# Halving the first and last unit by queries, maxima as bf16 trees, and eight-head projections spread by DMA, in a two-branch attention kernel

## The chip, the core and the metric

The kernel runs on one core of one Trainium2 chip. A core has five engines, each with its own instruction stream: TensorE (PE in the profile, its weight loads PEld), VectorE (DVE), ScalarE (ACT), GpSimd (POOL) and SyncE (SP), whose stream here only issues DMAs. Operands lie in SBUF; TensorE writes its products to PSUM, eight banks of 128×512 f32. The metric is the device time of one execution in microseconds (us), as the median of several; smaller is better.

## The reference

Two independent attention branches of 32 heads with 16 dimensions each, sequence S = 2048, width 512, bf16 inputs; their outputs are concatenated.

```python
# A: softmax attention
q, k, v = split_heads(x @ wqkv)                  # 32 heads, 16 dimensions
p = softmax(einsum("bhqd,bhkd->bhqk", q, k) * 16 ** -0.5)
a = merge(einsum("bhqk,bhkd->bhqd", p, v)) @ wo
# B: linear attention with a learnt feature map
q, k, v = split_heads(x2 @ wqkv2)
pq, pk = q @ w_phi, k @ w_phi                    # per head, 16 x 16
phi_q = concat([softmax(pq), softmax(-pq)])      # 32 features; phi_k alike
kv, z = phi_k^T v, sum_s(phi_k)
b = merge((phi_q kv) / (phi_q z + 1e-6)) @ wo2
out = concatenate([a, b], axis=-1)
```

Branch A forms 32 score maps of 2048×2048. Branch B never forms a score map; its softmax over 16 features needs, for each position and head, the largest and the smallest of 16 values.

## The kernel before

The heads of A go in eight groups `g` of four. A head's 16 dimensions are padded to 32 rows, so four heads fill the 128 rows of a column block of `QT` and `KT` (both `[128, group, S]`). A unit `u = (g, c)` is one group with one block `c` of 512 queries: 32 units, `c` outermost. Each unit is computed in two passes.

*First pass, the maxima.* A unit has 32 steps. A step is two matmuls of `emit_m1` (L889), which write scores of two heads for 128 queries by 512 keys into two of PSUM's banks 0 to 3, and one reduction r1 of `emit_r1` (L903), by which DVE takes the maximum over the 512 keys of each. When a segment's steps are done, `emit_mchain` reduces the four partial maxima (L913, DVE), POOL negates them and splits them into a high and a low bf16 half (L918, L920, L921), SP transposes them by a DMA into `mcols` (L923) and copies them by two DMAs into rows 16 and 17 of each head in `QT` (L926). The same rows of `KT` hold ones, so that the second pass subtracts the maximum inside its matmul.

*Second pass, the exponentials.* Eight steps after its end (`LAGX`), a segment's blocks begin, 64 for a whole unit: a block is one score matmul M2 of one head, 128 keys by 512 queries, into one of the three ring banks 4 to 6 (L954), and one exponential of ScalarE from PSUM into a slot of `pT` (L960, 15 slots). Four blocks later `pv_go` multiplies by V with a column of ones (L1008, four column groups of TensorE, bank 7), so that the sums of the exponentials come out beside the products. After a unit, ScalarE evacuates bank 7 to `X`, and SP and POOL form reciprocals (L1117 DMA, L1122 power on POOL, DMAs L1124 and L1127) and multiply (L1137) into `QT`, which serves as storage of the normalised output; later jobs project it with `WOp` (L820) and store it.

A unit in `SPLIT` (0 and 31) goes as two segments of two heads with all 512 queries. In PV each such segment fills only two column groups; in unit 0, 64 matmuls of zeros fill the others, and in the last unit additional matmuls with ones make the sums (64 rows × 512 columns each).

*Projections.* `proj` projects x for one group and one 512-block (L457), four matmuls with zero-padded weights `WQp`, `WKp`, which DVE fills at the start by two memsets (L304, L305) and two copies (`pad_copy`, L312). ScalarE evacuates into `KT` with a bias that sets the rows of ones (L469), or into `QT` (L433). Groups 2 to 7 need 24 K jobs and 6 Q jobs from slot 30 on, every four slots; the Q jobs of the other query blocks follow from slot 200, every 16.

*Branch B* runs as background jobs. `fm(n)`, n = 0 to 31, starts at slot 172 + 26n: 128 positions of the 512 features of K (n below 16) or Q. The job's matmuls (L583) are evacuated by ScalarE to `pB` (L433, f32), `red` takes maximum and minimum on DVE (L593, L596), `sub` subtracts both on POOL (L603, L605), ScalarE exponentiates (L611), POOL sums (L618 to L629), takes reciprocals by a power (`rec`, L641) and multiplies (L661); matmuls, transposes, a power for the denominators (L769) and the output copy L800 follow.

*What sets the order.* A planner, written in Python, simulates the engines with fixed costs (the class `_Clock`, its object `ck`) and lays down each engine's instruction order. In each turn it picks a step, a block, a piece of a background job (`jobs`, each with a first slot and a due slot `by`), a PV, or matmuls of zeros (L1086, L1101), which keep TensorE busy. `later(slot, fn)` runs `fn` at a given step; `pool_slot` keeps POOL free around a segment's end; `ck.extra` charges DVE for work beside r1. Waits are semaphores derived from the dependencies. SP takes its instructions in order: a DMA that has to wait for its data holds up what follows it.

*The end.* After the last r1 come the remaining blocks. `emit_acc` lays down, seven matmuls at a time, the projection of seven groups of the last four output tiles (L1152); before the last unit's normalisation three bursts stand in the planned order without a place in the planner's time, the fourth is in `emit_last`. That function then forms reciprocals as exp(−ln(sum)) on ScalarE (L1167, L1171), multiplies on DVE (L1176), adds the eighth group (L1183) and stores (L1191).

Of the kernel before, what the change touches and what calls it, by code (L numbers as in the profile page):

```python
# [148 lines left out]
def bass_concat_heads__softmax_full_mha__linear_kernel_hedgehog__prompt_kernel(  # L149
# [7 lines left out]
    NG = 8  # L157
# [4 lines left out]
    SPLIT = {0, NU - 1}  # L162
# [20 lines left out]
    for u in range(NU):  # L183
        segs += [(u, (0, 1)), (u, (2, 3))] if u in SPLIT else [(u, (0, 1, 2, 3))]
# [3 lines left out]
    for v, (u, rows) in enumerate(segs):  # L188
        steps = [(v, rows[i] // 2, qt, kc) for kc in range(NKC) for qt in range(4) for i in range(0, len(rows), 2)]
        if u == 0 and v == 1:  # L190
            order[4:4] = steps[0:4]
            steps = steps[4:]
        order += steps
    steps_of = [[q for q, o in enumerate(order) if o[0] == v] for v in range(NV)]
    seg_end = [qs[-1] + 1 for qs in steps_of]
    of_b = [v for v in range(NV) for _ in range(NKT * len(segs[v][1]))]
    seg_b = [of_b.index(v) for v in range(NV)]
    LAG = seg_end[0] + LAGX

    with contextlib.ExitStack() as es:  # L200
# [33 lines left out]
        WQp = sb("WQp", [128, 4, NG, 128], BF)  # L234
        WKp = sb("WKp", [128, 4, NG, 128], BF)
# [15 lines left out]
        pB = sb("pB", [128, 2, 512], F32)  # L251
# [3 lines left out]
        mB = sb("mB", [128, 2, 2, 32], F32)  # L255
# [48 lines left out]
        t_wq0 = P.op("dve", lambda e: e.memset(wqf.bitcast(U32), 0))  # L304
        t_wk0 = P.op("dve", lambda e: e.memset(wkf.bitcast(U32), 0))  # L305
# [3 lines left out]
        def pad_copy(dst, col0, dep0):  # L309
            src = wA[:, :, col0:col0 + 512].rearrange("p ct (gr d) -> p ct gr d", d=16)  # L310
            dv = dst[:].rearrange("p ct g (r x) -> p ct (g r) x", x=32)[:, :, :, 0:16]
            return P.op("dve", lambda e: e.tensor_copy(dv, src), [t_wa[col0 // 512], dep0])  # L312

# [3 lines left out]
        t_stage0 = P.op("pool", lambda e: e.memset(flat(stage).bitcast(U32), 0), [t_wkp])  # L317
        t_bd0 = P.op("pool", lambda e: e.memset(flat(BD).bitcast(U32), 0))
        t_wo0 = P.op("pool", lambda e: e.memset(flat(WOp).bitcast(U32), 0))
        t_vp1 = P.op("pool", lambda e: e.memset(VP[:, :, :, 16:17], 1.0))  # L320
        t_yd1 = P.op("pool", lambda e: e.memset(Yd[:], 1.0))
        t_vb1 = P.op("pool", lambda e: e.memset(vB[:], 1.0))
# [37 lines left out]
        def add_job(slot, pieces, fin, by=None, when=None):  # L360
            by = slot + BY if by is None else by
            njobs[0] += 1
            jobs.append((by, slot, njobs[0], pieces, fin, when))

        def next_job(tau):

            return min((j for j in jobs if j[1] <= tau and (j[5] is None or j[5]())), default=None)
# [9 lines left out]
        def bg_at(tau):  # L377
# [5 lines left out]
            if j is None or not ring_free:  # L383
                return None
# [941 lines left out]
```

## Time and profile before

| what | value |
|---|---|
| median of 3 runs | 1284.21 us (1283.9 to 1286.1) |
| the profiled execution's own time | 1283.74 us |
| its span, first to last instruction | 1282.0 us |
| TensorE's granted clock | 0.998 |
| VectorE busy | 1214.9 us, 95%, of it r1 (L903) 1170.2 |
| ScalarE busy | 1180.3 us, 92%, of it exponentials (L960) 1062.0 |
| TensorE busy | 1219.7 us, 95%, of it matmuls of zeros 581.9 + 146.7 |
| GpSimd busy | 600.8 us, 47% |
| DMA | 26.69 MB, 21 GB/s on average |

The page of the profile gives for one execution each engine's busy time with its share of the span, a strip of 40 slices with the busy share in tenths, and the costliest groups of instructions, one line each: source line and engine, operation, output<-inputs with partitions × elements, the count; then the busy time and the mean of one in ns; then the engine's idle time just ahead of these instructions and what ended most of it. Timelines list instructions in order of time: start, duration, engine, line, and in square brackets the idle time before with its releaser. SPq is SyncE's DMA queue.

### The profile page before, as it was taken

To read this page: it belongs to the slowest core of one execution; us is meant where nothing else is said; L and a number is where in the kernel's file an instruction comes from. 1 tells how busy PE (TensorE), PEld (TensorE's weight loads), DVE (VectorE), ACT (ScalarE), POOL (GpSimd) and SP (SyncE) were. 2 spreads that over 40 slices of the span, in tenths; PEclk is the share of its full clock that TensorE was granted. 3 is DMA by queue.
4 is the path that set the end of the run, shared out by engine and by line. 5 is a ranking of instruction groups with operands and counts; after the bars stand their busy time and mean duration, and the time that the engine had idled before them with its cause. 6 is when DMAs were issued, how large, how long until landed. Compare 5 with 4: busy or idle time off the path is not lost.

```text
span 1282.0 us, 28798 instructions
## 1 busy us (share of the span) xinstructions
PE 1219.7 (95%) x12059; PEld 408.0 (32%) x12059; DVE 1214.9 (95%) x1132; ACT 1180.3 (92%) x2321; POOL 600.8 (47%) x620
## 2 busy tenths in 40 slices
PE   8999999999999999999999999999999999999998
PEld 2223333333332233333333333333333233333333
DVE  8999999999999999999999999999999999999920
ACT  3789999999998999999999899999999999999986
POOL 2000102544655565546646346556555554646640
PEclk9999999999999999999999999999999999999999
DMA  6212200000001000000001110112211202121110
GB/s 132 60 16 40 35 7 4 7 7 7 7 6 19 6 8 7 7 6 3 7 7 7 23 24 11 31 19 20 32 19 27 36 15 32 23 24 19 29 20 21
DMA packets 75209, 26.69 MB, mean 21 GB/s; under 512 B 65928, under 2 KB 73096, under 8 KB 75080
## 3 DMA queue, kind: packets, MB, share of 16 engines
q1 hardware_dynamic: 73736, 23.56, 13.6%
q8 instruction: 94, 1.54, 0.5%
q10 hardware_dynamic: 1344, 1.31, 0.3%
q14 instruction: 35, 0.29, 0.1%
HBM read 3.16 MB, written 4.19 MB: 6 GB/s over the span
## 4 chain that ended last, share of the span: by engine, by line
ACT 51%; PE 27%; DVE 21%; issue 1%; DMA 0%; SPq 0%; ACTq 0%
ACT pT L960 45%; DVE part L903 20%; PE PS L954 7%; PE PS L889 4%; PE PS L457 3%; PE PS L1101 3%; PE PS L1008 2%; PE PS L583 2%; ACT eB L611 1%; PE PS L445 1%; PE PS L793 1%; PE PS L684 1%; ACT X L433 1%; ACT pB L433 1%; PE PS L1152 1%
## 5 line engine op out<-in xcount | busy, mean ns | idle before, releaser
L903 DVE TENSOR_REDUCE part<-PS 128x2 f32<-128x1024 f32 x1024 | 1170.2, 1215 | 5.7 <-PE PS L889 2.2
L960 ACT ACTIVATE pT<-PS 128x512 bf16<-128x512 f32 x2048 | 1062.0, 637 | 67.2 <-PE PS L954 27.0
L954 PE MATMUL PS<-QT,KT 32*128 32x512 bf16 x2048 | 657.1, 384 | 18.1 <-ACT pT L960 2.6
L1086 PE MATMUL PS<-zmv,ones_t 32*128 32x512 bf16 x1745 | 581.9, 382 | 0.3 <-ACT X L433 0.2
L889 PE MATMUL PS<-KT,QT 32*128 32x512 bf16 x2048 | 447.3, 383 | 14.1 <-DVE part L903 10.6
L954 PEld LDWEIGHTS PS<-QT,KT 32*128 32x128 bf16 x2048 | 176.9, 91 | 400.0 <-ACT pT L960 243.7
L1008 PE MATMUL PS<-pT,VP 128*17 128x512 bf16 x2048 | 210.7, 384 | 9.9 <-ACT pT L960 0.8
L918 POOL TENSOR_SCALAR stage<-mrow 128x16 bf16<-128x16 f32 (+1 forms) x34 | 8.8, 259 | 332.9 <-DVE mrow L913 332.9
L1101 PE MATMUL PS<-zmv,ones_t 128*17 128x256 bf16 x3028 | 146.7, 276 | 1.5
L1086 PEld LDWEIGHTS PS<-zmv,ones_t 32*128 32x128 bf16 x1745 | 143.3, 91 | 1.7 <-ACT X L433 1.1
L889 PEld LDWEIGHTS PS<-KT,QT 32*128 32x128 bf16 x2048 | 97.5, 91 | 122.3 <-DVE part L903 90.3
L1122 POOL TENSOR_TENSOR lr<-lr,neg 128x16 f32<-128x16 f32 x31 | 90.1, 2906 | 80.6 <-DMA lr<-X 80.5
L1008 PEld LDWEIGHTS PS<-pT,VP 128*17 128x17 bf16 x2048 | 51.4, 87 | 130.2 <-issue 69.3
L769 POOL TENSOR_TENSOR den_t<-den_t,neg 128x32 f32<-128x32 f32 x16 | 87.1, 5445 | 1.3
L641 POOL TENSOR_TENSOR wB<-wB,neg 128x32 f32<-128x32 f32 x16 | 87.0, 5440 | 0.8
L1101 PEld LDWEIGHTS PS<-zmv,ones_t 128*17 128x17 bf16 x3028 | 60.5, 90 | 80.4 <-issue 70.2
L1137 POOL TENSOR_TENSOR QT<-X,Yd 128x256 bf16<-128x256 f32 x62 | 43.8, 728 | 55.7 <-DMA Yd<-Yd 55.7
L618 POOL TENSOR_TENSOR sB<-eB 128x512 f32<-128x512 bf16 x32 | 36.9, 1154 | 67.3 <-ACT eB L611 67.3
L661 POOL TENSOR_TENSOR wA<-eB,rB 128x512 bf16<-128x512 bf16 x64 | 67.0, 1069 | 1.6
L603 POOL TENSOR_TENSOR uB<-pB,mB 128x512 f32<-128x512 f32 x32 | 33.9, 1060 | 52.0 <-DVE mB L593 52.0
L1176 DVE TENSOR_TENSOR QT<-PS,Yd 128x256 bf16<-128x256 f32 x2 | 0.8, 419 | 52.4 <-ACT Yd L1171 52.4
L583 PE MATMUL PS<-WKp,xBT 128*128 128x512 bf16 x128 | 38.0, 384 | 1.7 <-ACT pT L960 0.2
(85 smaller groups left out, 671.5 us busy)
## 6 DMA issues: line engine op xcount, KB each, us to landing
Yd<-Yd SPq DMA_DIRECT2D x124, 32.0 KB, 3.2
out_dram<-xAT SPq DMA_DIRECT2D x16, 128.0 KB, 1.8
out_dram<-OA SPq DMA_DIRECT2D x12, 128.0 KB, 1.7
wA<-in_A_wqkv_dram ACTq DMA_DIRECT2D x2, 512.0 KB, 5.1
QT<-mcols SPq DMA_DIRECT2D x60, 4.0 KB
mcols<-stage SPq DMA_TRANSPOSE x34, 2.3
wA<-in_A_wqkv_dram SPq DMA_DIRECT2D x1, 512.0 KB, 4.3
WOp<-in_A_wo_dram SPq DMA_DIRECT2D x4, 128.0 KB, 4.2
```

The source lines that it names most:

```text
L583: add_job(slot, mm_pieces(lambda e, b, ct: e.matmul(PS[:, b, :], xBT[:, ct, st * 128:(st + 1) * 128], Wf[:, x, ct, :], start=(ct == 0), st ...
L641: t = P.op("pool", lambda e: e.tensor_tensor(wB[:, n % 4, :], wB[:, n % 4, :], neg1[:, 0:1].broadcast_to([128, 32]), ALU.pow), [cx["r"], t ...
L661: t = P.op("pool", lambda e, a=a: e.tensor_tensor(f4[:, :, a, :], e4[:, :, a, :], r2[:, :, 1 - a].unsqueeze(2).broadcast_to([128, H, 16]), ...
L769: cx["rd"] = P.op("pool", lambda e: e.tensor_tensor(den_t[:, :], den_t[:, :], neg1[:, 0:1].broadcast_to([128, 32]), ALU.pow), [t, t_neg])
L889: tok = P.op("pe", lambda e, r=r, bank=2 * (q1 % 2) + i: e.matmul(PS[:, bank, :], QT[32 * r:32 * r + 32, g, q0:q0 + 128], KT[32 * r:32 * r ...
L903: r1[q1] = P.op("dve", lambda e: e.tensor_reduce(part[:, u % 2, 2 * pr:2 * pr + 2, qt, kc], PS[:, b:b + 2, :], AX.X, ALU.max), deps)
L954: m2_t[B] = P.op("pe", lambda e: e.matmul(PS[:, bank, :], KT[32 * r:32 * r + 32, g, kt * 128:(kt + 1) * 128], QT[32 * r:32 * r + 32, g, c ...
L960: exp_t[B] = P.op("act", lambda e: e.activation(pT[:, slot, :], PS[:, bank, :], ACT.Exp, scale=0.25), [m2_t[B], slot_reader.get(slot)])
L1008: tok = P.op("pe", lambda e, B=B, r=r: e.matmul(PVB[32 * r:32 * r + 17, :], VP[:, kt, 4 * g + r, :], pT[:, B % RING, :], start=(kt == 0), ...
L1086: fill_tok[0] = P.op("pe", lambda e: e.matmul(PS[:, 7, :], ones_t[32 * r:32 * r + 32, :], zmv[32 * r:32 * r + 32, :], start=False, stop=Fa ...
L1101: P.op("pe", lambda e, cq=cq: e.matmul(PS[32 * cq:32 * cq + 17, bank, 0:256], ones_t[:, 0:17], zmv[:, 0:256], start=(bank != 7), stop=(ban ...
L1122: rec = P.op("pool", lambda e: e.tensor_tensor(lr[:, ub, :], lr[:, ub, :], neg1[:, 0:1].broadcast_to([128, 16]), ALU.pow), [lr_t[u], t_neg])
```

## The change

Four edits in one.

The first and the last unit are halved by queries: each segment has all four heads and 256 queries. An M2 block then holds two key tiles of 256 columns as two matmuls, PV and the sums of the last unit take 256 columns for four heads (128 rows), and the matmuls of zeros in unit 0 go.

`pB` and `mB` become bf16. `red` does nothing for the first of two maps; for the second it takes maximum and minimum of both by trees, halving 16 values in four steps, eight `tensor_tensor` in place of four `tensor_reduce`; the two subtractions follow one after the other.

The projections of groups 2 to 7 use weights without padding, eight heads (two groups) in one job: 24 jobs in place of 48. ScalarE evacuates into `oct_t` (two buffers), and eight DMAs on SP's queue, 16 rows × 512 columns each, spread the heads to their rows in `QT` or `KT`, whose other rows POOL presets at the start. POOL copies the unpadded weights (`rest_copy`); the padding for groups 0 and 1 stays on DVE. Jobs come every 6 slots, later every 24.

The seven-group sums of three of the last output tiles become jobs of the planner, each matmul a piece, with a fixed bank; `emit_last` runs once they are done.

```diff
-    SPLIT = {0, NU - 1}
+    SPLIT = {0: (2, 2), NU - 1: (2, 2)}
...
-        segs += [(u, (0, 1)), (u, (2, 3))] if u in SPLIT else [(u, (0, 1, 2, 3))]
+        q0 = 0
+        for nq in SPLIT.get(u, (4,)):
+            segs.append((u, q0, nq))
...
+        steps = [(v, pr, qt, kc) for kc in range(NKC) for qt in range(q0, q0 + nq) for pr in range(2)]
...
-        WQp = sb("WQp", [128, 4, NG, 128], BF)
-        WKp = sb("WKp", [128, 4, NG, 128], BF)
+        WQp = sb("WQp", [128, 4, 1024], BF)
+        WKp = sb("WKp", [128, 4, 1024], BF)
+        oct_t = sb("oct_t", [128, 2, 512], BF)
...
-        pB = sb("pB", [128, 2, 512], F32)
+        pB = sb("pB", [128, 2, 512], BF)
...
-        mB = sb("mB", [128, 2, 2, 32], F32)
+        mB = sb("mB", [128, 2, 2, 32], BF)
...
+        t_wq0 = P.op("dve", lambda e: e.memset(WQp[:, :, 0:256].bitcast(U32), 0))
+        t_wk0 = P.op("dve", lambda e: e.memset(WKp[:, :, 0:256].bitcast(U32), 0))
...
+        def rest_copy(dst, col0):
+            return P.op("pool", lambda e: e.tensor_copy(dst[:, :, 256:640], wA[:, :, col0 + 128:col0 + 512]),
+                        [t_wa[col0 // 512]])
...
         t_stage0 = P.op("pool", lambda e: e.memset(flat(stage).bitcast(U32), 0), [t_wkp])
+        t_wqr = rest_copy(WQp, 0)
+        t_wkr = rest_copy(WKp, 512)
         t_bd0 = P.op("pool", lambda e: e.memset(flat(BD).bitcast(U32), 0))
         t_wo0 = P.op("pool", lambda e: e.memset(flat(WOp).bitcast(U32), 0))
         t_vp1 = P.op("pool", lambda e: e.memset(VP[:, :, :, 16:17], 1.0))
         t_yd1 = P.op("pool", lambda e: e.memset(Yd[:], 1.0))
+        t_kt1 = P.op("pool", lambda e: e.memset(KT[:, 2:NG, :], 1.0))
+        t_qt0 = P.op("pool", lambda e: e.memset(QT[:, 2:NG, :].bitcast(U32), 0))
...
+        d_oct = [dsem("oct0"), dsem("oct1")]
+        oct_d = {}
+        n_oct = [0]
...
+            at = g if g < 2 else 1 + g // 2
             pieces = mm_pieces(lambda e, b, ct: e.matmul(
-                PS[:, b, :], wpad[:, ct, g, :], xAT[:, ct, c * 512:(c + 1) * 512],
-                start=(ct == 0), stop=(ct == 3)), [t_xa[c], t_wqp if kind == "q" else t_wkp])
+                PS[:, b, :], wpad[:, ct, 128 * at:128 * at + 128], xAT[:, ct, c * 512:(c + 1) * 512],
+                start=(ct == 0), stop=(ct == 3)),
+                [t_xa[c], (t_wqp if g < 2 else t_wqr) if kind == "q" else (t_wkp if g < 2 else t_wkr)])
...
+                if g >= 2:
+
+                    i = n_oct[0] % 2
+                    n_oct[0] += 1
+                    t = aevac(oct_t[:, i, :], PS[:, b, :], [tok, oct_d.get(i)])
+                    dst, dep = (QT, t_qt0) if kind == "q" else (KT, t_kt1)
+                    for gg in range(2):
+                        for r in range(4):
+                            oct_d[i] = P.dma("sp", d_oct[i], lambda e, gg=gg, r=r: e.dma_start(
+                                dst[32 * r:32 * r + 16, g + gg, sl],
+                                oct_t[64 * gg + 16 * r:64 * gg + 16 * r + 16, i, :]), [t, dep])
+                    for gg in range(2):
+                        (qt_ready if kind == "q" else kt_ready)[(g + gg, c)] = oct_d[i]
+                    return t
...
         at = 30
-        for g in range(2, NG):
+        for g in range(2, NG, 2):
             for t in group(g):
                 add_job(at, *proj(*t), by=at + 10)
-                at += 4
+                at += 6
         at = 200
         for c in range(1, NQC):
-            for g in range(NG):
+            for g in (0, 1, 2, 4, 6):
                 add_job(at, *proj("q", g, c), by=at + 30)
-                at += 16
+                at += 24
...
             def red(tau):
-                cx["mx"] = P.op("dve", lambda e: e.tensor_reduce(mB[:, i, 0, :], p3, AX.X, ALU.max),
-                                [cx["p"]] + use(("m", i)))
-                ck.extra += 1.19
-                cx["mn"] = P.op("dve", lambda e: e.tensor_reduce(mB[:, i, 1, :], p3, AX.X, ALU.min), [cx["p"]])
-                s = pool_slot(tau + 2, 2)
-                later(s, lambda: sub(s))
+                if i == 0:
+                    first_map[:] = [cx, sub]
+                    return
+                pp = pB[:].rearrange("p a (h f) -> p (a h) f", f=16)
+                for k, op in ((0, ALU.max), (1, ALU.min)):
+                    t3 = uB[:, 0, 256 * k:256 * k + 256].bitcast(BF).rearrange("p (h f) -> p h f", f=8)
+                    t = P.op("dve", lambda e, t3=t3, op=op: e.tensor_tensor(t3, pp[:, :, 0:8], pp[:, :, 8:16], op),
+                             [cx["p"], first_map[0]["p"]] + use(("u", 0)))
+                    for w in (4, 2):
+                        t = P.op("dve", lambda e, t3=t3, op=op, w=w: e.tensor_tensor(
+                            t3[:, :, 0:w], t3[:, :, 0:w], t3[:, :, w:2 * w], op), [t])
+                    t = P.op("dve", lambda e, t3=t3, op=op, k=k: e.tensor_tensor(
+                        mB[:, :, k, :].unsqueeze(3), t3[:, :, 0:1].rearrange("p (a h) f -> p a h f", a=2),
+                        t3[:, :, 1:2].rearrange("p (a h) f -> p a h f", a=2), op),
+                        [t] + use(("m", 0)) + use(("m", 1)))
+                ck.extra += 1.62
+                cx["mx"] = cx["mn"] = first_map[0]["mx"] = first_map[0]["mn"] = t
+                s = pool_slot(tau + 3, 2)
+                later(s, lambda fn=first_map[1]: fn(s))
+                s2 = pool_slot(s + 2, 2)
+                later(s2, lambda: sub(s2))
...
-                    QT[32 * rows[0] + 16 + hl:32 * rows[-1] + 32:32, g, c * 512:(c + 1) * 512],
+                    QT[16 + hl:128:32, g, c * 512 + qs * 128:c * 512 + (qs + nq) * 128],
...
-            m2_t[B] = P.op("pe", lambda e: e.matmul(
-                PS[:, bank, :], KT[32 * r:32 * r + 32, g, kt * 128:(kt + 1) * 128],
-                QT[32 * r:32 * r + 32, g, c * 512:(c + 1) * 512],
-                start=True, stop=True, tile_position=(32 * r, 0)),
-                [bank_reader.get(bank), mr_t[v], kt_ready[(g, kt // 4)]])
+            lo, w = c * 512 + qs * 128, nq * 128
+            for j in range(per):
+                m2_t[B] = P.op("pe", lambda e, j=j: e.matmul(
+                    PS[:, bank, j * w:j * w + w], KT[32 * r:32 * r + 32, g, (kt + j) * 128:(kt + j + 1) * 128],
+                    QT[32 * r:32 * r + 32, g, lo:lo + w],
+                    start=True, stop=True, tile_position=(32 * r, 0)),
+                    [bank_reader.get(bank), mr_t[v], kt_ready[(g, kt // 4)]] if j == 0 else [],
+                    signal=(j == per - 1))
...
-            if not last:
-                for cq in [r for r in range(4) if r not in rows]:
-                    P.op("pe", lambda e, cq=cq: e.matmul(
-                        PS[32 * cq:32 * cq + 17, 7, :], ones_t[:, 0:17], zmv[:, :],
-                        start=False, stop=False, tile_position=(0, 32 * cq), skip_group_check=True),
-                        deps, signal=False)
+            lo, w = qs * 128, nq * 128
+            tok = None
+            for j in range(per):
+                for B in Bs:
+                    r = blk[B]
+                    tok = P.op("pe", lambda e, B=B, r=r, j=j: e.matmul(
+                        PVB[32 * r:32 * r + 17, lo:lo + w], VP[:, kt + j, 4 * g + r, :],
+                        pT[:, B % RING, j * w:j * w + w],
+                        start=(first and j == 0), stop=(kt + j == NKT - 1), tile_position=(0, 32 * r),
+                        skip_group_check=True),
+                        deps, signal=(B == Bs[-1] and j == per - 1))
...
-                    later(tau + 4 + 2 * k, lambda k=k: emit_acc(k, k + 1, [mul_t[u], r1[total_q1 - 1], t_wo]))
+                    slot = max(tau + 4, total_q1 + 1) + 3 * k
+                    add_job(slot, *acc_job(k, [mul_t[u], t_wo, r1_last]), by=slot + 4, bank=k + 1)
...
+        def acc_job(k, deps):
             st = 4 * (NQC - 1) + k
-            for i in range(NG - 1):
-                P.op("pe", lambda e, i=i: e.matmul(
-                    PS[:, bank, :], QT[:, i, st * 128:(st + 1) * 128], WOp[:, i, :],
-                    start=(i == 0), stop=False), deps if i == 0 else [], signal=False)
-            acc_t[k] = bank
+
+            def piece(i):
+                return mm_piece(1, lambda e, b, i: e.matmul(
+                    PS[:, b, :], QT[:, i, st * 128:(st + 1) * 128], WOp[:, i, :],
+                    start=(i == 0), stop=False), lambda: [d() if callable(d) else d for d in deps], first=i)
+
+            def fin(b, tok, tau):
+                acc_t[k] = b
+            return [piece(i) for i in range(NG - 1)], fin
```

Left out are the same segment arithmetic in `block_at`, `pv_at`, `emit_mchain` and the fill, the sums of the last unit, which are split like PV, and `pad_copy` with only 128 source columns.

## The prediction

> **What bounds the kernel now.** I read, in this order, the page's busy times and slices, the costliest groups, a table of busy time by stage, the timelines of DVE and of the DMA queue, and last ScalarE's and TensorE's timelines behind DVE's end.
>
> The page's busy times and slices: VectorE, TensorE and ScalarE all look full.
>
> ```profile
> PE 1219.7 (95%) x12059; PEld 408.0 (32%) x12059; DVE 1214.9 (95%) x1132; ACT 1180.3 (92%) x2321; POOL 600.8 (47%) x620
> ...
> DVE  8999999999999999999999999999999999999920
> ACT  3789999999998999999999899999999999999986
> ```
>
> TensorE's figure says little: 1745 + 3028 of its matmuls (lines L1086, L1101) multiply zeros. In the costliest groups DVE's own work has almost no idle time ahead of it:
>
> ```profile
> L903 DVE TENSOR_REDUCE part<-PS 128x2 f32<-128x1024 f32 x1024 | 1170.2, 1215 | 5.7 <-PE PS L889 2.2
> ...
> L769 POOL TENSOR_TENSOR den_t<-den_t,neg 128x32 f32<-128x32 f32 x16 | 87.1, 5445 | 1.3
> ```
>
> The table by stage (busy time and count of each engine, granted clock, DMA share, GB/s) gives the two stages that matter:
>
> ```profile
> core 0: us, PE busy (x) PEld busy (x) DVE busy (x) ACT busy (x) POOL busy (x), PEclk, DMA share, GB/s
> 800.00:1000.00 200.00, 190.81 (x2041) 66.06 (x2041) 199.46 (x188) 195.39 (x395) 115.50 (x119) 1.00 0.18 24
> ...
> 1224.00:1282.00 58.00, 52.87 (x590) 19.80 (x589) 2.39 (x6) 42.53 (x86) 12.06 (x10) 0.99 0.11 20
> ```
>
> Up to 1224 us DVE bounds (199.46 of 200): whatever it gains or loses before that moves the end by as much. Then it is done, and 58 us of tail hang on ScalarE with TensorE. So an edit is priced by two questions: does it change DVE's time before 1224, or the tail behind it?
>
> **The trees (first-map wait, eight `tensor_tensor`).** DVE's timeline in front of one of today's maps (start, busy):
>
> ```profile
> 1109.46 0.21 DVE L913 TENSOR_REDUCE mrow<-part 128x16 f32<-128x64 f32 x1
> 1109.59 0.68 DVE L593 TENSOR_REDUCE mB<-pB 128x32 f32<-128x512 f32 x1
> 1110.18 0.68 DVE L596 TENSOR_REDUCE mB<-pB 128x32 f32<-128x512 f32 x1
> 1110.77 9.13 DVE L903 TENSOR_REDUCE part<-PS 128x2 f32<-128x1024 f32 x8
> ```
>
> From start to start two reduces take 1110.77 − 1109.59 = 1.18 us; 32 maps are 37.8 us, which go. L913 takes 0.13 us for 64 elements, L593 0.59 for 512: 1.03 ns an element and 0.063 fixed. The new bursts, one for two maps, are 16, each of two trees that write 512, 256, 128 and 64 elements: 2 × (960 elements + 4 fixed). At 1.03 ns that is 2.5 us, 40.0 in all: 2.2 lost. The fastest bf16 row of DVE is a copy:
>
> ```profile
> L312 DVE COPY WKp<-wA 128x2048 bf16<-128x2048 bf16 x1 | 0.7, 694 | 1.4 <-DMA wA<-in_A_wqkv_dram 1.4
> ```
>
> (694 − 63) / 2048 = 0.31 ns an element; at that the bursts cost 1.09 each, 17.5, a gain of 20.3. No row has a bf16 operation with two inputs on DVE. I take half the copy's rate, since two operands are read for each element written: 0.62 ns, 1.69 us a burst, 27.0 in all. **−10.8 us**, ends −20.3 and +2.2.
>
> The Trainium skill ("VectorE: DVE Perf Modes", the perf-mode tier table) gives tensor_tensor twice the fp32 rate for bf16 in SBUF and the reduce no faster mode; by it I estimate 1.5 us a burst and −13.8 us. No row here shows it for two inputs.
>
> The first map of a pair now waits for the second, and its later steps (subtraction on POOL L603, exponential L611, sums L618) start later. Both maps' work stays ahead of its use: the last maximum stands 43 r1 reductions before DVE's end instead of 44.
>
> **DVE beside POOL.** The trees read two SBUF operands while POOL works; every DVE row of this trace up to 1224 us reads one operand, so no row prices a wait of one engine for the other. POOL is busy 115.50 of 200 us, and its longest operations are the powers L641, L769 and L1122: 87.0 + 87.1 + 90.1 = 264 us in operations of 2.9 to 5.4 us. If a burst had to wait out a running POOL operation, the mean of half a length, weighted by time, is about 0.7 us a burst, 11 us for 16; if at several of its eight, 2.3, 37 us. Zero is the other end. I take 0, because the two small reduces above, which read SBUF beside POOL, keep their pace, and hold the wait as a rival.
>
> **The eight-head projections.** For groups 2 to 7 one job makes eight heads unpadded, ScalarE evacuates once, and eight DMAs of 16×512 bf16 spread it: 24 jobs, 192 DMAs more on SP's queue, which handles its instructions in order. Per pair of jobs saved ScalarE drops one evacuation of about 0.6 us; 16 us in all, and TensorE 96 matmuls × 0.216 = 21 us. Both lie under DVE's bound: 0 (cover: r1; if it were gone, they would be a gain).
>
> What SP does early is not covered. Of its timeline (start, time in the queue):
>
> ```profile
> 41.82 3.66 SPq L517 DMA_DIRECT2D BD<-in_B_w_phi_dram  x8
> ...
> 55.71 7.70 SPq L529 DMA_TRANSPOSE wA<-in_B_wqkv_dram  x6
> ...
> 87.24 1.10 SPq L923 DMA_TRANSPOSE mcols<-stage  x1
> ...
> 89.49 1.17 SPq L926 DMA_DIRECT2D QT<-mcols  x2
> ...
> 101.46 10.86 SPq L533 DMA_TRANSPOSE xBT<-in_B_x_dram  x8
> ...
> 124.02 1.52 SPq L923 DMA_TRANSPOSE mcols<-stage  x1
> ...
> 142.20 2.48 SPq L1127 DMA_DIRECT2D Yd<-Yd  x4
> ```
>
> The maxima of a unit go through L923 and L926 into QT, and its score blocks (L954) wait for them; with no block, no exponential, the three-bank ring and the planned order of TensorE stall, r1's matmuls stand behind the waiting block, and DVE with them. From job K(2,3) to unit 2's maxima SP now has: its evacuation at about 75.3 us; then the weight transposes 5 × 1.28, xBT 9 × 1.36, a lr read 0.6, unit 1's maxima chain 3.4 (87.24 to 90.66), the Yd chain 4.65: 27.3; and eight jobs' 64 new DMAs. A plain 16-partition DMA takes 3.66 / 8 = 0.457 (BD); that gives 29.2 more and an end at 131.8, against 124.02 before, with 0.5 us to spare: **+7.3**. The low end is 0.39 a DMA (an output store issues in 0.35), +3; the high end Yd's SBUF-to-SBUF 2.48 / 4 = 0.62, +17.8. I take BD's, nearest in shape; Yd's chain also carries its wait for L1122. The wait of r1's matmul at step 64 for Q(2,0), whose eight DMAs queue there too, is the same lateness (2 to 4 of the 7), and so is oct_t's: an evacuation waits for the DMAs of two jobs earlier, and stands in front of ScalarE's exponentials. Behind unit 3 the queue has drained: a unit lasts 36.6 us, a job's DMAs 3.7. From slot 200 a job comes every 24 steps, 27 us.
>
> **The start.** POOL copies the rest of the weights (2 × 128×4×384) ahead of the ones of VP (before at 10.11–12.37; the first evacuation into VP is at 14.54), then presets KT and QT (estimates 10.8 and 5.4 us by the memsets' pace). POOL was idle from 20.75 to 36.01, when the first maxima chain needs it. The copies take 1.35 (0.88 ns an element) to 3.2 us (2.07, the row of L603) each: **+0.3**, 0 to +3. DVE's smaller memsets and copies bring nothing: the first K matmul waited for xAT, landed at 8.74, when WKp was ready at 7.90.
>
> **The tail.** ScalarE's and TensorE's timelines behind DVE's end (start, busy, idle before and its releaser):
>
> ```profile
> 1250.22 1.57 ACT L960 ACTIVATE pT<-PS 128x512 bf16<-128x512 f32 x3 [1.65 <-PE PS L954]
> ...
> 1253.66 2.16 ACT L960 ACTIVATE pT<-PS 128x512 bf16<-128x512 f32 x4 [1.87 <-PE PS L954]
> ...
> 1258.14 0.60 ACT L960 ACTIVATE pT<-PS 128x512 bf16<-128x512 f32 x1 [2.31 <-PE PS L954]
> ```
>
> ```profile
> 1251.63 1.68 PE L1152 MATMUL PS<-WOp,QT 128*128 128x512 bf16 x7
> ```
>
> The holes ahead of the tail's exponentials sum to 10.6 us; the three above (5.8) stand behind bursts like L1152's, seven matmuls in 1.68 us. Planned piece by piece they still cost TensorE's time, of which I take 1.9 less to show. Of the other 4.8 us, 3.8 go: four blocks' PV and sums now take 0.43 us of TensorE instead of 0.86, and the zero matmuls are gone. Against this 80 blocks instead of 75 follow the last r1 (5 × 0.49 = +2.45), two more evacuations of B's folded weights (2 × 0.37 = +0.75); B's last output, which is copied in ScalarE's wait of 0.93 before the closing logarithm, moves ahead of it (−0.5, an estimate). Together **−3**, from −7 to +3. First unit: its halves have the same 32 steps and 64 blocks; its M2 splits cost TensorE time under DVE's bound, 0.
>
> **Sum.** −10.8 + 7.3 + 0.3 − 3.0 = −6.2. The profiled execution took 1283.74 us (span 1282.0), 0.47 under the median of 1284.21: 1277.5, on the median's basis 1278.
>
> **The rivals.**
>
> *R1, POOL's port or a like wait makes the trees slow.* It ends slower. For it: POOL is busy 58% of the time and its powers last 5.4 us; bursts 9, 11 and 14 of the planned order stand next to L769's. Against it: no wait of DVE is seen beside POOL today. From 6.2 + 2.6 = 8.8 us, 0.55 us a burst, it decides for slower; at 0.7 it gives 1289, at 2.3 a burst 1315.
>
> The Trainium skill ("SBUF — State Buffer", who interferes with whom) lets a DVE instruction with two SBUF inputs and a GpSimd one that reads SBUF block each other for the whole instruction; by that rule the time is this rival's. No row of this trace has such a DVE instruction of any length.
>
> *R2, the spreading DMAs cost Yd's 0.62 us.* +10.5 more: 1288. For it: the same shape and route. Against: Yd's holds a wait.
>
> *R3, the trees run unpacked*, at 1.03 ns an element: +13.0, 1291. Against: the copy's 0.31 on bf16.
>
> *R4, SP is not late*, because planned blocks absorb it or the DMAs go at 0.39, or the tail gives all its 7: 1264 to 1271.
>
> **Chances.** My forecast (1271 to 1281.5) 0.42, R1 0.25, R2 0.17, R3 0.05, R4 0.11. About 0.2%, 2.6 us, is what a measurement can tell from no change. The forecast's upper edge and mild cases of R1 and R2 lie within it: 0.13. Faster: 0.52; slower: 0.35. The range cuts R1's far end and R4's: 1266 to 1296; the forecast's own is 1271 to 1281.5.
>
> **What would show it.** DVE's rows of the trees: 1.7 us a burst and no gap inside is my case; rows of several us, or gaps beside POOL's powers, R1; 2.5 us, R3. DVE's idle time ahead of r1 between 80 and 140 us: about 7 us, released by TensorE that waited for QT from the DMA queue; near 17 for R2, near 0 for R4. The queue's time of one spreading DMA: 0.46. In the tail, ScalarE's holes: near 5 us instead of 10.6. Wrong in kind I would be if DVE had idle time all through the span, for a cause in the planned order that the instruction order alone does not tell.

## The result, and the profile after

The changed kernel takes 1354.3 us in the median (1349.5 to 1357.3) against 1285.2: 1.0535 times as long, 95% interval 1.0501 to 1.0569. I had forecast 1278. Ratios are formed from the executions of a kernel that lie within 1.5% of its fastest. The page of its profiled execution (1357.3 us):

```profile
span 1355.5 us, 29490 instructions
...
PE 1261.4 (93%) x12283; PEld 402.6 (30%) x12283; DVE 1222.5 (90%) x1196; ACT 1176.0 (87%) x2297; POOL 617.7 (46%) x624
...
DVE  7978789989999999999979999889989999999840
...
PEclk9988888978999999999969999789969999989799
...
L961 DVE TENSOR_REDUCE part<-PS 128x2 f32<-128x1024 f32 x1024 | 1176.5, 1218 | 70.2 <-PE PS L947 29.4
```

L961 is r1 (before L903): the idle time ahead of it went from 5.7 to 70.2 us, and it waits for TensorE. The strip PEclk, the clock granted to TensorE, was nines throughout before; its mean fell from 0.998 to 0.928. DVE is done at 1303.1 instead of 1224.4 us, 78.7 later; the tail behind it is 5.2 shorter (52.4 instead of 57.6); together the span's 73.5.

Where DVE lost them: up to 220 us it has done 155 r1 instead of 181, 26 × 1.143 = 30 us; behind 268 us, where the first trees come, its idle time of over 0.2 us at a time sums to 37.0; the trees themselves take 44.7 where the reductions took 37.8. The table by stage shows both kinds of loss (columns as in the prediction; the third from the end is the granted clock):

```profile
core 0: us, PE busy (x) PEld busy (x) DVE busy (x) ACT busy (x) POOL busy (x), PEclk, DMA share, GB/s
80.00:90.00 10.00, 4.00 (x48) 1.25 (x43) 5.29 (x5) 4.48 (x9) 0.00 (x0) 0.88 0.15 36
...
100.00:110.00 10.00, 7.74 (x48) 1.68 (x47) 5.13 (x5) 5.01 (x10) 1.99 (x1) 0.56 0.18 42
140.00:150.00 10.00, 3.23 (x28) 0.91 (x24) 4.94 (x5) 4.06 (x8) 0.00 (x0) 0.78 0.19 43
...
670.00:680.00 10.00, 9.90 (x82) 2.78 (x78) 8.12 (x8) 7.03 (x15) 5.38 (x4) 0.56 0.04 8
690.00:700.00 10.00, 10.00 (x58) 1.92 (x54) 6.44 (x7) 6.63 (x13) 0.00 (x0) 0.50 0.01 2
```

At 80 and 140 us TensorE stands idle. At 670 to 700 it looks full, but at half its clock, with fewer matmuls, and DVE gets too little. TensorE's timeline names what it waited for:

```profile
90.65 0.61 PE L947 MATMUL PS<-KT,QT 32*128 32x512 bf16 x2 [3.90 <-DMA QT<-oct_t]
102.26 0.61 PE L1015 MATMUL PS<-QT,KT 32*128 32x512 bf16 x2 [2.26 <-DMA QT<-mcols]
...
151.19 0.58 PE L1015 MATMUL PS<-QT,KT 32*128 32x512 bf16 x1 [7.79 <-DMA QT<-mcols]
...
472.65 0.39 PE L947 MATMUL PS<-KT,QT 32*128 32x512 bf16 x2 [0.94 <-DVE part L961]
...
669.50 0.39 PE L947 MATMUL PS<-KT,QT 32*128 32x512 bf16 x2 [1.00 <-DVE part L961]
...
671.43 0.60 PE L1065 MATMUL PS<-pT,VP 128*17 128x512 bf16 x4
```

The first three are the early kind: spreading DMAs and maxima that come late out of SP's queue. The row at 669.50 is the later kind: a burst of trees has ended at 668.2, TensorE had nothing left to do, stood idle 1.00 us, and two microseconds later a matmul takes 0.60 us instead of 0.39. Full clock is back at about 702 us: from the table's shares (0.56, 0.50, 0.50 and 0.90 in 700 to 710) some 31 us at one half. The clock was halved within 8 us of the start of nine of the 16 bursts, beside idle times of TensorE between 0.6 and 2.1 us; behind the burst at 468.80 an idle time of 0.94 us (the row at 472.65) had no such effect. What decides between the two is not shown.

SP's timeline, for the early kind (start, time in the queue; L499 spreads, L981 and L984 bring the maxima):

```profile
77.60 5.01 SPq L499 DMA_DIRECT2D KT<-oct_t  x8
...
84.35 5.01 SPq L499 DMA_DIRECT2D QT<-oct_t  x8
...
97.74 1.12 SPq L981 DMA_TRANSPOSE mcols<-stage  x1
...
138.75 5.01 SPq L499 DMA_DIRECT2D KT<-oct_t  x8
...
146.41 1.24 SPq L981 DMA_TRANSPOSE mcols<-stage  x1
```

A job's eight DMAs take 5.01 us, 0.626 each. Unit 1's maxima start 10.5 us later than before (87.24), unit 2's 22.4 later (124.02).

DVE's timeline of one burst, the same in 12 of 16 to 0.04 us:

```profile
273.52 0.42 DVE L641 TENSOR_TENSOR uB<-pB 128x512 bf16<-128x512 bf16 x1
273.97 0.61 DVE L644 TENSOR_TENSOR uB<-uB 128x256 bf16<-128x256 bf16 x2
274.62 0.27 DVE L646 TENSOR_TENSOR mB<-uB 128x64 bf16<-128x64 bf16 x1
...
276.10 5.74 DVE L961 TENSOR_REDUCE part<-PS 128x2 f32<-128x1024 f32 x5
```

From 273.52 to 276.10 it is 2.58 us, where the planner charges 1.62.

### The profile page after: what moved, and what is told of

Same layout as the page of the kernel before. It is cut to its first block, busy times and chain, and to the rows that moved or that the text cites. A ratio compares the mean times of both kernels' runs of the same rounds, so it can differ in the third digit from the quotient of the medians.

```text
span 1355.5 us, 29490 instructions
## 1 busy us (share of the span) xinstructions
PE 1261.4 (93%) x12283; PEld 402.6 (30%) x12283; DVE 1222.5 (90%) x1196; ACT 1176.0 (87%) x2297; POOL 617.7 (46%) x624
## 4 chain that ended last, share of the span: by engine, by line
DVE 33%; ACT 30%; PE 29%; SPq 4%; DMA 2%; issue 1%; POOL 0%; ACTq 0%
DVE part L961 30%; ACT pT L1022 27%; PE PS L1015 9%; PE PS L947 5%; PE PS L1164 4%; PE PS L1065 3%; SPq L499 3%; PE PS L483 2%; DVE uB L644 1%; PE PS L1149 1%; PE PS L470 1%; PE PS L624 1%; DMA mcols<-stage 1%; ACT eB L668 1%; PE PS L850 1%
## 5 line engine op out<-in xcount | busy, mean ns | idle before, releaser
L961 DVE TENSOR_REDUCE part<-PS 128x2 f32<-128x1024 f32 x1024 | 1176.5, 1218 | 70.2 <-PE PS L947 29.4
L1015 PE MATMUL PS<-QT,KT 32*128 32x512 bf16 (+1 forms) x2176 | 675.0, 393 | 29.3 <-DMA QT<-mcols 12.3
L1149 PE MATMUL PS<-zmv,ones_t 32*128 32x512 bf16 x1745 | 618.3, 404 | 0.1
L947 PE MATMUL PS<-KT,QT 32*128 32x512 bf16 x2048 | 478.4, 407 | 34.2 <-DVE part L961 25.7
L1065 PE MATMUL PS<-pT,VP 128*17 128x512 bf16 (+1 forms) x2176 | 213.3, 393 | 13.1 <-ACT pT L1022 5.2
L1164 PE MATMUL PS<-zmv,ones_t 128*17 128x256 bf16 x3092 | 162.8, 296 | 3.2 <-ACT X L454 2.3
L947 PEld LDWEIGHTS PS<-KT,QT 32*128 32x128 bf16 x2048 | 100.3, 92 | 150.2 <-DVE part L961 112.8
L660 POOL TENSOR_TENSOR uB<-pB,mB 128x512 f32<-128x512 bf16 x32 | 33.5, 1048 | 60.1 <-DVE mB L646 60.1
```

The lines of the kernel that those rows point to most:

```text
L947: tok = P.op("pe", lambda e, r=r, bank=2 * (q1 % 2) + i: e.matmul(PS[:, bank, :], QT[32 * r:32 * r + 32, g, q0:q0 + 128], KT[32 * r:32 * r ...
L961: r1[q1] = P.op("dve", lambda e: e.tensor_reduce(part[:, u % 2, 2 * pr:2 * pr + 2, qt, kc], PS[:, b:b + 2, :], AX.X, ALU.max), deps)
L1015: m2_t[B] = P.op("pe", lambda e, j=j: e.matmul(PS[:, bank, j * w:j * w + w], KT[32 * r:32 * r + 32, g, (kt + j) * 128:(kt + j + 1) * 128], ...
L1065: tok = P.op("pe", lambda e, B=B, r=r, j=j: e.matmul(PVB[32 * r:32 * r + 17, lo:lo + w], VP[:, kt + j, 4 * g + r, :], pT[:, B % RING, j * ...
L1149: fill_tok[0] = P.op("pe", lambda e: e.matmul(PS[:, 7, :], ones_t[32 * r:32 * r + 32, :], zmv[32 * r:32 * r + 32, :], start=False, stop=Fa ...
L1164: P.op("pe", lambda e, cq=cq: e.matmul(PS[32 * cq:32 * cq + 17, bank, 0:256], ones_t[:, 0:17], zmv[:, 0:256], start=(bank != 7), stop=(ban ...
```

## The experiments

My theory after reading the two traces: two separate causes, both through TensorE's clock. (S) the spreading DMAs make SP's queue late; (T) the bursts take DVE longer than the planner knows, TensorE's planned order runs dry, and the half clock that follows costs more than the burst. Rivals: one early disturbance with everything behind it as its consequence, or the trees' own time and waits beside POOL.

### Undoing one part, the other, and both

The reductions back, on the bf16 maps, one map at a time:

```diff
-                    t = P.op("dve", lambda e, t3=t3, op=op: e.tensor_tensor(t3, pp[:, :, 0:8], pp[:, :, 8:16], op),
-                             [cx["p"], first_map[0]["p"]] + use(("u", 0)))
...
+                cx["mx"] = P.op("dve", lambda e: e.tensor_reduce(mB[:, i, 0, :], p3, AX.X, ALU.max),
+                                [cx["p"]] + use(("m", i)))
+                ck.extra += 1.19
+                cx["mn"] = P.op("dve", lambda e: e.tensor_reduce(mB[:, i, 1, :], p3, AX.X, ALU.min), [cx["p"]])
```

> The changed kernel with the four reductions per pair of maps in place of the trees (on bf16 maps, charged 1.19 us per map as before); the eight-head projections with their 192 DMAs stay. Theory, two separate causes: the late queue of SP costs some 30 us up to 220 us (26 reductions fewer done by then x 1.143), the bursts with their half clock the rest, so this one is near 1284 + 30 - 5 (tail) = 1310, its clock near 0.97, and it has no clock drop behind 268 us. Rival, one cause: the early disturbance also brings the later drops; then it stays at 1345 or more. Rival, trees alone: it falls to 1285.

Measured: 1308.4 us (1307.1 to 1320.9); clock 0.984. Behind 268 us the clock drops in one slice of 10 us only (0.88 at 300 to 310), where I had expected none.

The padded projections back (weights, jobs and slots of before; no `oct_t`, no presets), the trees kept:

```diff
-                ck.extra += 1.62
+                ck.extra += 1.7
...
-            at = g if g < 2 else 1 + g // 2
             pieces = mm_pieces(lambda e, b, ct: e.matmul(
-                PS[:, b, :], wpad[:, ct, 128 * at:128 * at + 128], xAT[:, ct, c * 512:(c + 1) * 512],
+                PS[:, b, :], wpad[:, ct, g, :], xAT[:, ct, c * 512:(c + 1) * 512],
```

> The changed kernel with the projections of before (48 padded jobs, no spreading DMAs); the trees stay, charged 1.7 us in the plan instead of 1.62. Theory, two separate causes: r1 has the pace of before up to the first burst, then bursts cost 45 - 38 = 7 us and the half clock behind them some 39: 1284 + 46 - 5 = 1325, with drops right behind bursts. Rival, one cause (the early disturbance): near 1286.

Measured: 1328.8 us (1319.7 to 1343.1). In its profiled execution the clock was halved within 8 us of the start of five of the 16 bursts.

Both edits at once:

> Both undone: what is left of the change is the halving by queries and the planned sums of the last tiles. My prediction's tail: -3 (-7 to +3), so 1281; the tail measured in the changed kernel (52.4 us behind DVE's end instead of 57.6) says 1279. Rival, the halving itself disturbs the first unit: over 1287.

Measured: 1281.3 us (1279.3 to 1282.4), 0.9968 of the kernel before (0.9956 to 0.9980).

From 1281.3 the eight-head projections add 27, the trees 48, both together 73: two separate causes, as S and T have it; the early disturbance does not carry the later one. What is left of the change, the halving and the planned sums, gains 4 us.

### Is it the planner's charge?

```diff
-                ck.extra += 1.62
+                ck.extra += 2.9
```

> The changed kernel with one number different: the planner charges a burst 2.9 us instead of 1.62, near the 2.6 to 4.2 that the bursts take. Theory (TensorE runs out of planned work during a burst, falls idle and loses half its clock): the drops behind 268 us go and with them most of 39 us: about 1320. Rival, the bursts' own time or a wait beside POOL is what costs: within 10 us of 1354.

Measured: 1324.1 us (1323.4 to 1338.0). One number changed gives 30 us back. In this run's table by stage the clock behind 268 us falls below 0.95 in one place only (380 to 400 us); in the changed kernel it did so in more than twenty slices of 10 us.

The same without trees, in the kernel before: the two reductions of each second map are done twice, in one run without a charge (shown) and in the other with 1.19 in the place of 0.0.

```diff
+                if i == 1:
+                    for _ in range(1):
+                        P.op("dve", lambda e: e.tensor_reduce(mB[:, i, 0, :], p3, AX.X, ALU.max), [cx["mx"]], signal=False)
+                        cx["mx"] = cx["mn"] = P.op(
+                            "dve", lambda e: e.tensor_reduce(mB[:, i, 1, :], p3, AX.X, ALU.min), [cx["mn"]])
+                    ck.extra += 0.0
```

> The kernel before, with the two reductions of each second map done twice and nothing charged for it in the plan: 16 times some 1.2 to 1.4 us more on DVE that TensorE's order does not know of, as with the trees (2.6 to 4.2 taken, 1.62 charged). Theory (unplanned DVE time lets TensorE run dry and halves its clock): more than the 16 x 1.3 = 21 us, with half-clock stretches behind some of them: 1315 to 1345. Rival (a stretch of DVE only costs its own length): 1306.

Measured: 1327.4, 1336.1, 1347.6 and 1355.0 us in four executions; the ratio, from the two shortest, is 1.0369 (1.0326 to 1.0411), some 47 us.

> The same doubled reductions with 1.19 us charged for each pair in the plan. Theory: the clock stays near 1.0 and the cost is the time itself: 1285 + 21 = 1306, some 10 to 40 us under the unplanned one. Rival: no different from the unplanned one.

Measured: 1305.6 us (1302.0 to 1310.8). The strips of the granted clock, without and with the charge:

```profile
PEclk9999999997999899999899979998999899999999
```

```profile
PEclk9999999999999999999999999999999999999999
```

The same work costs 20.7 us where the plan knows of it (16 × 1.29) and some 47 where it does not (42 to 70 in the single executions). This shows T's mechanism in a kernel that has neither trees nor spreading DMAs.

### What the trees cost by themselves

> The changed kernel's trees, chained as they are, with the projections of before and 2.7 us charged for a burst (1.7 charged: 1328.8). Theory (the own price of the trees is 44 - 38 = 6 us, the rest was the unplanned time): 1281.3 + 6 = 1287, with up to 10 more where a burst meets POOL. Rival (the bursts cost much more than their length, planned or not): over 1305.

The edit is `ck.extra += 2.7` in place of 1.7 in the kernel with trees and padded projections. Measured: 1292.4 us, 1.0059 (1.0044 to 1.0074); 48 us over "both undone" became 11. The bursts sum to 44.3 us, 6.5 over the reductions; three of them took 3.4 to 4.1 us, and behind the last of these the clock was halved again.

Can the order within a burst make it shorter?

```diff
-                for k, op in ((0, ALU.max), (1, ALU.min)):
...
+                for w in (8, 4, 2, 1):
+                    for k, op in ((0, ALU.max), (1, ALU.min)):
...
-                ck.extra += 1.62
+                ck.extra += 2.1
```

> The changed kernel with the loads moved as in the run before and the two trees of a burst interleaved (maximum, minimum, maximum, ...), charged 2.1 us. Theory A (an operation of a tree waits some 0.2 us for the write of the one before): interleaved, a burst takes 1.6 to 1.9 us instead of 2.58, 16 of them 26 to 30 us under the reductions' 38, and the time is 1270 to 1280, under both kernels. Rival B (each small operation has a fixed price of some 0.25 us however it is ordered): still about 2.6 us a burst, 1290 to 1300.

Measured: 1305.1 us (1303.6 to 1313.1), no faster than the same kernel with reductions (below, 1305.0): the time misses the theory. The burst is what theory A said: 1.80 us in most cases, 30.2 for all.

> The changed kernel with the projections of before and the trees of a burst interleaved, charged 2.0 us (1.80 measured for 14 of 16 bursts in the run before, 30.2 us for all against 37.8 for the reductions). Theory: the queue's lateness is gone with the spreading DMAs and the bursts are within what the plan charges, so the clock stays near 1.0 and the time is the 1281.3 of both parts undone less 7.6: 1273.7, under both kernels. Rival (any burst of about 2 us that TensorE cannot use costs more than its own length, planned or not): 1281 or more.

Measured: 1287.6 us (1280.2 to 1292.9), ratio 1.0009 (0.9989 to 1.0030): a miss again. Three of its 16 bursts took 2.84, 2.99 and 2.67 us, each beside a POOL multiplication (the one at 804.34 beside QT<-X,Yd, 1.60 us from 804.63). Behind the first two the clock was halved, at 506 and at 810 us, behind the third it was not; a further drop at 1240 us stands behind no burst. So the bursts were put where the plan has POOL free:

```diff
+                at = pool_slot(tau, 2)
+                if at == tau:
+                    burst(at)
+                else:
+                    later(at, lambda: burst(at))
```

> The interleaved trees with the projections of before (1287.6), each burst put at a slot in which the plan has no POOL operation, charged 2.1 us. Theory (a tree beside a POOL multiplication such as QT<-X,Yd takes 2.7 to 3.0 us instead of 1.80, which the plan does not know, and the half clock behind it takes the gain back): 16 bursts of 1.8 us, no half clock behind them, 1273 to 1278, under both kernels. Rival (a burst costs as such): 1285 or more.

Measured: 1277.9 us (1277.0 to 1278.2), 0.9945 of the kernel before (0.9933 to 0.9958). A burst of this run on DVE's timeline:

```profile
677.24 0.75 DVE L623 TENSOR_TENSOR uB<-pB 128x512 bf16<-128x512 bf16 x2
677.91 0.86 DVE L627 TENSOR_TENSOR uB<-uB 128x256 bf16<-128x256 bf16 x4
678.67 0.45 DVE L630 TENSOR_TENSOR mB<-uB 128x64 bf16<-128x64 bf16 x2
679.04 1.22 DVE L945 TENSOR_REDUCE part<-PS 128x2 f32<-128x1024 f32 x1
```

All 16 take 1.79 to 1.92 us, 29.1 together, and the clock is 0.999. DVE ends 9.9 us before that of "both undone" (1218.9 against 1228.8 us), of which the tail gives 4.8 back (56.7 behind DVE's end against 51.9). This version beats the kernel before and the changed one.

### What the spreading DMAs cost

```diff
-            later(48 + 3 * i, lambda i=i: load_wt(i))
+            later(99 + 3 * i, lambda i=i: load_wt(i))
-            later(72 + 3 * i, lambda i=i: load_xb(i // 4, i % 4))
+            later(123 + 3 * i, lambda i=i: load_xb(i // 4, i % 4))
```

> The kernel with the four reductions per pair and the spreading DMAs (1308), with branch B's 8 weight transposes moved from steps 48-69 to 99-120 and its 16 xBT loads from 72-117 to 123-168, so that SP has only the spreading DMAs and the maxima's chains in the early window. Theory (SP's queue is late because 24 loads of 1.3 us stand between 64 DMAs of 0.63): the clock stays at 1.0 between 80 and 220 us and the time falls to 1281 to 1288. Rival (the spreading DMAs alone are too many, 15 jobs x 5.0 = 75 us beside the chains): over 1300.

Measured: 1305.0 us (1300.0 to 1310.7), a miss: 3 us gained. Unit 2's maxima came at 129.4 instead of 146.4 us and TensorE no longer waited for them, but it still waited for Q(2,0), and then 6.15 us for unit 3's maxima, now behind the moved loads.

```diff
-            for t in group(g):
+            for t in group(g)[0:1] + group(g)[4:5] + group(g)[1:4]:
                 add_job(at, *proj(*t), by=at + 10)
-                at += 6
+                at += 8
...
+            later(60 + 5 * i, lambda i=i: load_wt(i))
+            later(100 + 4 * i, lambda i=i: load_xb(i // 4, i % 4))
```

> The kernel with the four reductions and the spreading DMAs, with each group pair's Q job moved from fifth to second place, jobs every 8 slots instead of 6, the weight transposes at steps 60 to 95 and the xBT loads at 100 to 160. Theory (all that the spreading DMAs cost is lateness in SP's queue; where nothing waits for it they cost nothing and the ScalarE and TensorE time that they save is hidden): the clock stays at 1.0 and the time is 1279 to 1284, that of both parts undone. Rival (the queue stays too full, 15 jobs x 5.0 us beside 31 us of loads and the chains): over 1290.

Measured: 1319.8 us (1313.9 to 1323.1), a miss for the worse: TensorE waits 3.95, 4.10, 6.00 and 2.00 us for QT<-mcols, at 96, 140, 185 and 348 us. A job or two stood ahead of a unit's maxima.

```diff
+                    near = [q for q in seg_end if q - 6 <= tau <= q + 1]
+                    if near:
+                        held.append(1)
+                        later(near[-1] + 2, spread)
...
+                add_job(at, *proj(*t), by=at + 10, when=lambda: not held)
```

The last line keeps further projection jobs back while DMAs are held.

> The run with the reductions, the earlier Q jobs and jobs every 8 slots (1320), with one thing more: a job's eight spreading DMAs are not issued from 6 steps before a segment's end to 1 step behind it, but behind the maxima's DMAs. Theory (a unit's maxima come late because one or two jobs of 5.0 us stand in front of them in SP's order, not because the queue is full): no wait of TensorE for QT from mcols over 1 us, the clock at 1.0 behind 50 us, and 1279 to 1285. Rival (moved behind, they only make the next units' K or Q late): over 1295.

Measured: 1306.7 us (1302.0 to 1308.2), 1.0159 (1.0137 to 1.0181). The waits for QT<-mcols are gone, unit 1's maxima start at 87.26 as before the change; another wait has their place, which ScalarE's and then TensorE's timeline show:

```profile
98.61 0.60 ACT L454 ACTIVATE oct_t<-PS 128x512 bf16<-128x512 f32 x1 [10.43 <-DMA KT<-oct_t]
```

```profile
99.26 0.60 PE L1010 MATMUL PS<-QT,KT 32*128 32x512 bf16 x1 [6.69 <-ACT oct_t L454]
```

ScalarE stands 10.43 us before an evacuation that needs a buffer, its exponentials behind it, and TensorE behind these.

> The run with held DMAs (1306.7), with four buffers of oct_t instead of two, and 13 slots of pT instead of 15 to make room. Theory (holding the DMAs made ScalarE's evacuations wait for a buffer, 6.69 and 4.82 us of TensorE's idle time): both waits go and the time is 1281 to 1288. Rival (the next thing in line takes their place, since 64 DMAs and the loads fill the queue): 1295 or more.

The edits are four `oct_t` buffers with their semaphores instead of two, and `RING = 13`. Measured: 1300.1 us (1298.0 to 1317.7), 1.0109 (1.0092 to 1.0126): the rival. Both waits are gone in its profiled execution, the longest (1317.7), in which TensorE waits 6.52 us for QT<-mcols at 178.5 us; whether the shorter ones wait there too is not shown.

> The changed kernel with the four reductions (1308.4), in which each projection job issues only two of its eight spreading DMAs (those of the first head of each group): 48 instead of 192. The other heads of groups 2 to 7 keep the presets as K and Q, so the scores of these heads are left out; all instructions of the engines stay. Theory (the DMAs' 0.63 us each in SP's queue are the whole cost of the eight-head projections): 1280 to 1285, the clock at 1.0 between 80 and 220 us. Rival (something else of these projections costs, such as POOL's presets or their order): over 1295.

The edit is `for r in range(1)` instead of `range(4)` around the spreading DMA. Measured: 1286.0 us (1284.2 to 1287.7), 1.0005 (0.9995 to 1.0014). Taking away three quarters of the DMAs, and nothing else, takes away 22 of the 27 us; no slice between 50 and 280 us has a clock under 0.95. So the DMAs in SP's queue are the cost, or nearly all of it; what the other 5 us are is open. That an arrangement exists that hides all 192 I have not shown: four attempts left 19 to 39 us, and all kept the DMAs on SP's queue.

### The last edit alone

> The kernel before with the last edit alone: the seven-group sums as planned jobs, first and last unit still halved by heads. Both parts together gained 4.2 us. My prediction gave the sums 1.9 of the tail's gain and the halving 3.8 less 2.45 for its later blocks: 1283.0. Rival (the sums carry all of it): 1281; other rival (the halving carries all of it): 1285.

Measured: 1282.3 us (1280.6 to 1282.7), 0.9976 (0.9967 to 0.9985): 2.1 us for the planned sums, and by difference some 2 for the halving.

## Why the prediction was wrong

**The trees, −10.8.** They lost 6.9 us (44.7 against 37.8): the term was mis-sized in both its parts. The rate of 0.62 ns an element was too dear: (0.42 − 0.27) / 448 gives 0.33, close to the copy's 0.31, my low end. The fixed price of 0.063 us, taken over from reductions that wait for nobody, was far too cheap: 0.25 for an operation that needs the result of the one before. 2 × (960 × 0.33 ns + 4 × 0.25) = 2.63, measured 2.58. Interleaved, 1.80 us leave 0.15 each, so some 0.1 of it was the wait within the chain. Even my high end, 40.0 in all, was too low. That a burst is two chains of four dependent operations, one behind the other, stood in the diff.

**What failed altogether** is a step that I did not take: to hold the bursts' length against the planner's charge. I treated DVE as the only bound: "whatever it gains or loses before that moves the end by as much". The order of TensorE is laid down for the charge of 1.62; a burst of 2.58 or more leaves it idle, and with nine of the 16 bursts the clock was halved as well. I had named DVE idle time all through the span as what would show me wrong in kind, but given no price to it. That is 36 us of the trees' 48 (1328.8 against 1292.4).

The Trainium skill ("TensorE: Matmul & The Clock Gate", part 1) describes this gate: half rate by default or after an idle window of about 3.4 us, full rate after a busy window as long. The half rate agrees (0.50 granted). The lengths do not: here, behind bursts, idle times of 0.6 to 2.1 us went with it, and at 670 us it stayed for some 31 us with TensorE shown busy 99 to 100%.

**SP's queue, +7.3.** Measured 27 (1308.4 against 1281.3). The mechanism and the place were right (waits of TensorE for QT, DVE idle between 80 and 140 us), the price was not: 0.626 us a DMA, which is Yd's row and the rival R2's, not BD's 0.457. With it my own sum, 75.3 + 27.3 + 64 × 0.626, gives 142.7 for unit 2's maxima; they came at 146.4. But the rival's +17.8 us fell short of the 30 measured by 220 us, again for the half clock (0.56 at 100 to 110 us), and unit 1's chain and Q(2,0) were late on their own account, which I had counted into the same lateness.

**POOL's port, 0, and the rival R1.** Waits exist but sum to 3.6 us over four bursts (3.09, 3.61, 2.95 and 4.18 us, less 2.57 each), and POOL's powers, on which I had built the rival, cause none: four bursts beside powers of 2.9 to 5.45 us took 2.56 to 2.59. My evidence for 0, two reduces that read one operand each, did not bear on operations with two. DVE's and POOL's timelines of the changed kernel beside a power, and beside a multiplication:

```profile
1181.25 5.45 POOL L826 TENSOR_TENSOR den_t<-den_t,neg 128x32 f32<-128x32 f32 x1
...
1244.82 1.46 POOL L1200 TENSOR_TENSOR QT<-X,Yd 128x256 bf16<-128x256 f32 x2 [1.09 <-DMA Yd<-Yd]
```

```profile
1184.39 0.61 DVE L644 TENSOR_TENSOR uB<-uB 128x256 bf16<-128x256 bf16 x2
...
1244.93 1.49 DVE L644 TENSOR_TENSOR uB<-uB 128x256 bf16<-128x256 bf16 x2
```

The same two operations take 0.61 us inside a power of 5.45 and 1.49 beside the multiplication. The Trainium skill ("SBUF — State Buffer", who interferes with whom) has a DVE operation with two SBUF inputs wait for a GpSimd one that reads SBUF; the multiplication agrees, the power, whose operands are 128×32, does not. The small sum is not its whole price: in the interleaved run without a POOL-free slot the half clock followed two of three such bursts.

**The covers, 0.** ScalarE's and TensorE's savings gave nothing that could be measured: with a quarter of the DMAs the eight-head projections still stood 4.7 us over the padded ones. **The start, +0.3**: 34 r1 by 50 us in both, right.

**The tail, −3.** Measured −5.2 in the changed kernel; alone, halving and sums gain 4 us of the whole time. I had expected ScalarE's holes there to shrink from 10.6 to near 5 us; those ahead of exponentials sum to 3.7 (0.52, 0.76, 0.95, 0.95, 0.26, 0.22). Mechanism right, size a little low.

R3's 1291 was the trees' right sign for a wrong reason: it put the price on the elements, and it lies on the fixed part. That its 2.5 us a burst comes close to the 2.58 measured is luck.

## What to carry to other kernels

Where an order of instructions is planned ahead, time on an engine has two prices: its length if the plan knows it, and its length plus what the other engines lose if not; hold every new operation's real duration against the plan's charge first. Price a chain of small dependent operations by the operation, not by the element, and interleave independent chains. A queue that serves in order is judged by who stands behind each group of transfers, and moving the groups mostly moves the wait.

## What I had not expected of the hardware

A wait of TensorE of only 1.00 us was followed by some 31 us at half clock, in a stretch where it was never idle for long; the same 20.7 us of DVE work cost some 47 when unplanned, with single executions between 1327 and 1355 us. And a POOL power of 5.45 us does not hold up a DVE operation with two SBUF operands, where a multiplication on 128×256 more than doubles it.
